# A layer norm, attention and GELU layer on one core: another order of the first stage's tasks, and head stacks in one tile

## Chip, core and metric

The kernel runs on one core of a Trainium2 chip, as one program. The metric is the device time of one execution in microseconds (us). The engines are named as in the profile: PE is TensorE's matmul, PEld its weight loads, DVE is VectorE, ACT ScalarE, POOL GpSimd; SP (SyncE) issues every DMA of this kernel, in program order, and its queue appears as SPq.

## What is computed

x has 2048 rows of 512 values, there are 32 heads of 16, and the feed-forward part has 1792 hidden units. One layer norm feeds both branches:

```python
xn = _layernorm(x)                                   # no weights
qkv = xn @ wqkv                                      # 512 -> 3 * 512, heads of 16
p = softmax(q @ k.T * 16 ** -0.5);  att = (p @ v) @ wo
h = gelu(xn @ w1 + b1);             mlp = h @ w2 + b2
return x + att + mlp
```

## The kernel before

Values are kept as pairs of f16 numbers (a high and a low part), so that a product of two of them is three matmuls (`PAIRS`). Q and K of a head are written to a DRAM tensor `qk_d` with three copies of parts per value, and read back as *stacks*: 48 rows (16 values by 3) for each of the four heads of a group, in the tiles `qst` and `kst`. Rows 62 and 63 of each half of a `qst` tile hold the negated row maxima of the scores, split in two, so that the second score product already has the maximum taken off. There are 8 groups of 4 heads (`g`), 4 query blocks of 512 (`qb`), and 16 units in each, so 512 units `u`; `t = 4 g + qb` counts the *turns* of 16 units.

A unit has two halves of the softmax. `s_half` makes scores with the queries in the partitions (`pS`) and DVE takes their maxima (line 330, four a unit). When a turn is through, `store` turns the maxima with PE, writes them to `m_d` in DRAM and reads them back into the stack's rows (lines 361 and 366). LEAD = 19 units later `e_half` makes the same scores with the keys in the partitions (`pT`), ACT takes the exponential (line 381, four a unit), and `v_half` sums with V (`pV`). Between these, a unit holds some products of a filler (`pD`): the rest of the V and QK projections, then the MLP, then the output projection, in this order, each as soon as its inputs are there. A filler group of 12 products in two halves takes three units at pace 4. At the change from the projections to the MLP, and again to the output projection, `flush` puts out all that is still queued for POOL and SP. From the MLP on, `more_stacks` issues one block's stack of the group after next in each unit, until its eight are out.

The first stage runs ahead of the units. It loads x and the weights, normalises (`normal`, line 896 and what follows), turns x with PE (line 928), projects the first Q and K (`project0`, line 958) and 11 of 16 V tiles (`v_tile`, line 1053), sends Q and K through DRAM into the stacks (line 990), and makes the scores of the first 19 units. Its tasks are put into an order by `Plan`: each task has an engine, a guessed duration, what it comes after and a `tail`, and `run` always takes, of the tasks that could begin first, the one with the longest tail. Every engine then keeps that order. Where the plan sees a gap on PE ahead of the first score, `fill` puts in matmuls that only keep PE busy (line 1122).

Lines that the change touches: `project0` (958 to 990), `v_tile` (1053), the turn of the first maxima (1081 to 1093), the stacks (480 and 990), `store` (361, 366), the load of `b1` (1127), and the generator `rest`, which lists the filler of the first blocks. After the stage, `prepare` begins on DVE with the maximum of `b1` (line 1165).

Of the kernel before, what the change touches and what calls it, by code (L numbers as in the profile page):

```python
# [18 lines left out]
P = 128  # L19
# [3 lines left out]
DH = 16  # L23
# [14 lines left out]
NV = 11  # L38
VT = 2600, 8000
FINE = "fine"  # L40
# [10 lines left out]
def layer_kernel(ctx: ExitStack, tc: tile.TileContext, x, wqkv, wo, w1, b1, w2, b2, out):  # L51
# [4 lines left out]
    def pool(stack, name, bufs=1, space=None, side=None):  # L56
# [22 lines left out]

    kst, qst = ([[[const.tile([P, QB], F16, name=f"{x}st{i}_{p}_{b}") for b in range(NQB)] for p in range(2)]  # L80
                 for i in range(2)] for x in "kq")

    def clear(i, blocks=range(NQB)):
        for b in blocks:
            for p in range(2):
                nc.gpsimd.memset(kst[i][p][b].bitcast(F32), MROWS)
                nc.gpsimd.memset(qst[i][p][b].bitcast(F32), 0.0)

# [117 lines left out]
    class Plan:  # L206
# [97 lines left out]
    def flush():  # L304

        settle()
        while steps or extras or any(q[2] for q in queue):
# [4 lines left out]
            slot[0] += 1  # L312

    def s_mm(u, n, s):
# [7 lines left out]
        tiled(None, s, qs[p][qb][r, qt * P:(qt + 1) * P], ks[p][kb][r, :], True, True)  # L322

# [15 lines left out]
    def s_end(u):  # L339
# [4 lines left out]
        g, qb = divmod(t, NQB)  # L344
        qs = qst[g % 2]
        mneg = mnegs[t % 2]
# [3 lines left out]
        def store():  # L350

            pt = banks("S")
            for a in range(2):
                nc.tensor.matmul(pt[32 * a:32 * a + 32, :64], mneg[64 * a:64 * a + 64, :],
                                 ident[64 * a:64 * a + 64, 64 * a:64 * a + 64], start=True, stop=True)
            mhl = work.tile([64, 2, 64], F16, name="mhl", bufs=2)
            nc.vector.tensor_scalar_mul(mhl[:, 0], pt[:64, :64], 1.0 / MROW)
            nc.vector.scalar_tensor_tensor(mhl[:, 1], pt[:64, :64], 1.0 / MROW, mhl[:, 0], op0=ALU.mult, op1=ALU.subtract)
            given("dve", 300)
            for a in range(2):  # L360
                nc.sync.dma_start(m_d[t, :, :, 64 * a:64 * a + 64], mhl[32 * a:32 * a + 16])
            for p in range(2):
                for a in range(2):
                    h = 2 * p + a
                    dst = qs[p][qb][64 * a + 62:64 * a + 64, :].rearrange("r (t q) -> r t q", q=P)
                    nc.sync.dma_start(dst, m_d[t, 4 * h:4 * h + 4].rearrange("t r q -> r t q"))

        stores[t] = store

    def e_half(u, n):  # L370
# [6 lines left out]
        k0 = (kt % 4) * P  # L377
        tiled(None, st, kst[g % 2][p][kt // 4][r, k0:k0 + P], qst[g % 2][p][qb][r, :], True, True)
        pe = work.tile([P, QB], F32, name="pe", bufs=12)
# [93 lines left out]
    NU = NG * NQB * 16  # L473

    def stacks(g, w, blocks):
        for b in blocks:
            for p in range(2):
                for a in range(2):
                    h = 4 * g + 2 * p + a
                    nc.sync.dma_start((qst, kst)[w][g % 2][p][b][64 * a:64 * a + 48, :],  # L480
                                      qk_d[w, h * DH:(h + 1) * DH, :, b * QB:(b + 1) * QB].rearrange("d j n -> (d j) n"))


# [68 lines left out]

    def project(m, w, sb, wh, bank, early=False):

# [5 lines left out]
        def finish(pj):  # L560
            def put():
                nc.sync.dma_start(dst[:, w:w + 2, :], stg)
                nc.sync.dma_start(dst[:, 2 - 2 * w, :], stg[:, 0])

            stg = ph.tile([P, 2, QB], F16, name="stg", bufs=3)
            given("act", 600)
            if early or (w == 1 and not m):
                nc.scalar.activation(stg[:, 0], pj, AF.Copy)
                nc.vector.tensor_tensor(stg[:, 1], pj, stg[:, 0], op=ALU.subtract)
            else:  # L570
                pf = ph.tile([P, QB], F32, name="pf", bufs=2)
                nc.scalar.activation(pf, pj, AF.Copy)
                if not m:
                    nc.scalar.activation(stg[:, 0], pj, AF.Copy)
                    nc.gpsimd.tensor_tensor(stg[:, 1], pf, stg[:, 0], op=ALU.subtract)
                else:
                    hi = lambda: nc.gpsimd.tensor_scalar(stg[:, 0], pf, 1.0, 0.0, op0=ALU.mult, op1=ALU.add)
                    lo = lambda: nc.gpsimd.tensor_tensor(stg[:, 1], pf, stg[:, 0], op=ALU.subtract)
                    later(1, lambda: pooled((620, hi), (1160, lo), (0, lambda: later(2, put, True))), True)
                    return  # L580

            put()

# [188 lines left out]
    with ExitStack() as st1:  # L772
# [48 lines left out]
        def tile_in(t):  # L821
            def fn():
                xs[t] = raw(("xs", t), "xs", [P, D], 8)
                nc.sync.dma_start(xs[t], x[t * P:(t + 1) * P, :])
# [11 lines left out]
        def piece_in(key, src, after=()):  # L836
# [3 lines left out]
            return add("SP", 420, fn, after, take=[key], size=700)  # L840

# [40 lines left out]
        wvv = wqkv[:, 2 * D:3 * D].rearrange("(c p) n -> p c n", p=P)  # L882
        v_in = [piece_in(("wch", "v", i), wvv[:, :, i * W:(i + 1) * W]) for i in range(2)]
        x_in += [tile_in(t) for t in range(4, NT)]
# [4 lines left out]
        def normal(sb):  # L889
# [18 lines left out]
            for i in range(4):  # L908
                v = 4 * sb + i
                if i >= DVE_X[sb]:  # L910
                    out.append(add("ACT", 620, lambda v=v, i=i: nc.scalar.activation(
                        xs[v], xs[v], AF.Identity, scale=sd[:, 2, i:i + 1], bias=sd[:, 4, i:i + 1]), [b]))
# [49 lines left out]
        def project0(w, sb):  # L962
# [23 lines left out]
            got = []  # L986
            for p_ in range(2):
                for a_ in range(2):
                    h_ = 2 * p_ + a_
                    got.append(add("SP", 420, lambda p_=p_, a_=a_, h_=h_: nc.sync.dma_start(  # L990
                        (qst, kst)[w][0][p_][sb][64 * a_:64 * a_ + 48, :],
                        qk_d[w, h_ * DH:(h_ + 1) * DH, :, sb * QB:(sb + 1) * QB].rearrange("d j n -> (d j) n")), [a, b], size=48))
            return got
# [46 lines left out]
        for i in range(2):  # L1040
            hi, lo = (wvh[j][:, :, i * W:(i + 1) * W] for j in range(2))
            key = ("wch", "v", i)
            h = add("ACT", 1040, lambda hi=hi, key=key: nc.scalar.activation(hi, tl[key], AF.Copy, scale=inv_v[:, 0:1]), [chain])
            wv_ready.append(add("DVE", 1200, lambda hi=hi, lo=lo, key=key: nc.vector.scalar_tensor_tensor(
                lo, tl[key], inv_v[:, 0:1], hi, op0=ALU.mult, op1=ALU.subtract), [h], free=[key]))

# [43 lines left out]
        for k in range(4):  # L1090
            def fn(k=k):
                dst = qst[0][k // 2][0][64 * (k % 2) + 62:64 * (k % 2) + 64, :].rearrange("r (t q) -> r t q", q=P)
                nc.sync.dma_start(dst, m_d[0, 4 * k:4 * k + 4].rearrange("t r q -> r t q"))
            add("SP", 270, fn, put, size=4)
# [38 lines left out]
        def rest():  # L1133
# [318 lines left out]
```

## Time and profile before

| | us |
|---|---|
| median of 3 runs (1506.58 to 1510.22) | 1507.2 |
| the profiled execution's own time | 1507.74 |
| its span | 1506.0 |
| PE busy | 1475.0 (98%) |
| DVE busy | 1376.2 (91%) |
| ACT busy | 1266.5 (84%) |
| POOL busy | 662.8 (44%) |

PE's busy time counts a matmul as busy also while it runs at half clock, and matmuls overlap, so the share alone does not tell where time is lost. The number of exponentials in a stretch does: four are a unit. The stage before the units ends with the first `pT` matmul at about 99.9 us.

### The profile page before, as it was taken

How to read it: one execution, taken by the hardware profiler on the slowest of the kernel's cores; microseconds unless marked ns; L12 is line 12 of the kernel's file. 1: busy time of each engine (PE TensorE's matmuls, PEld its weight loads, DVE VectorE, ACT ScalarE, POOL GpSimd, SP SyncE). 2: the span in 40 equal slices, each digit the busy share in tenths (PEclk: the TensorE clock that was granted, in tenths of full speed). 3: DMA queues.
4: the chain of work that ended last, by engine and by line, in shares of the span. 5: the costliest groups of instructions: out<-in, count | busy, mean ns of one | idle time of the engine just before them, and what ended most of it. 6: DMA issues, size and time to landing. Idle time of an engine off the chain costs nothing.

```text
span 1506.0 us, 87998 instructions
## 1 busy us (share of the span) xinstructions
PE 1475.0 (98%) x40055; PEld 814.7 (54%) x40055; DVE 1376.2 (91%) x2306; ACT 1266.5 (84%) x2367; POOL 662.8 (44%) x687
## 2 busy tenths in 40 slices
PE   8989999998999999999999999999999999999998
PEld 4435555554555555555555555555555555555554
DVE  7779989998999999999999999999999999999923
ACT  6748888887899888899988889998888999888884
POOL 3201979423677411278731137873105777211210
PEclk8999999999999999999999999999999999999999
DMA  6741677223222211131121111121112210111432
GB/s 214 226 150 41 208 223 232 85 85 100 83 86 76 80 50 30 41 83 36 51 57 49 44 50 37 46 79 57 30 36 56 65 43 21 48 53 39 131 99 93
DMA packets 114414, 124.82 MB, mean 83 GB/s; under 512 B 24700, under 2 KB 86012, under 8 KB 114040
## 3 DMA queue, kind: packets, MB, share of 16 engines
q1 hardware_dynamic: 114040, 119.19, 26.5%
q8 instruction: 313, 5.13, 1.4%
q14 instruction: 61, 0.50, 0.1%
HBM read 81.66 MB, written 37.34 MB: 79 GB/s over the span
## 4 chain that ended last, share of the span: by engine, by line
PE 86%; DVE 8%; DMA 3%; issue 1%; ACT 1%; SPq 1%; DVEq 0%; ACTq 0%
PE pV L167 25%; PE pD L167 22%; PE pS L167 18%; PE pT L167 18%; DVE mt L330 7%; PE pT L958 2%; DMA m_d<-mhl 1%; DMA xs<-in_A_x_dram 1%; PE pD L958 1%; DVE ac L1326 0%; PE pT L928 0%; DMA qst<-m_d 0%; DVE bs L896 0%; DVE mneg L347 0%; SPq L990 0%
## 5 line engine op out<-in xcount | busy, mean ns | idle before, releaser
L330 DVE TENSOR_REDUCE mt<-pS 128x1 f32<-128x512 f32 x2029 | 1297.3, 684 | 60.8 <-PE pS L167 36.4
L381 ACT ACTIVATE pe<-pT 128x512 f32<-128x512 f32 x2048 | 1111.8, 599 | 191.8 <-PE pT L167 86.2
L167 PE MATMUL pV<-pe,vv 64*32 64x512 f32 x8192 | 1073.4, 595 | 0.7 <-issue 0.6
L167 PE MATMUL pT<-qst,kst 64*32 64x512 f16 x8192 | 711.8, 379 | 6.6 <-DMA qst<-m_d 5.5
L167 PE MATMUL pS<-kst,qst 62*32 62x512 f16 x8116 | 617.8, 379 | 9.2 <-DVE mt L330 6.1
L167 PEld LDWEIGHTS <-qst 62*32 62x32 f16 x8192 | 277.9, 92 | 230.5 <-issue 58.9
L167 PEld LDWEIGHTS <-kst 64*32 64x32 f16 x8192 | 278.9, 91 | 180.2 <-issue 77.7
L167 PE MATMUL pD<-xb,wc 64*32 64x512 f16 x5376 | 361.6, 378 | 0.0
L167 PE MATMUL pD<-w_s,g 64*32 64x512 f16 x5376 | 359.1, 377 | 0.0
L167 PEld LDWEIGHTS pV<-pe,vv 64*32 64x32 f32 x8192 | 181.8, 105 | 87.7 <-PE pV L167 2.7
L167 PE MATMUL pD<-xt,wqk_h 64*32 64x512 f16 x2304 | 151.0, 378 | 0.3 <-issue 0.3
L167 PEld LDWEIGHTS <-wc 64*32 64x32 f16 x5376 | 117.1, 92 | 42.6 <-issue 0.3
L167 PEld LDWEIGHTS <-g 64*32 64x32 f16 x5376 | 113.1, 91 | 44.2
L1294 POOL TENSOR_TENSOR xa<-xa,yt 128x512 f32<-128x512 f32 x16 | 20.4, 1277 | 242.4 <-ACT yt L1292 242.4
L437 POOL TENSOR_TENSOR osb<-osb,rb 128x512 f32<-128x512 f32 x31 | 39.9, 1287 | 171.8 <-DMA rb<-den_d 116.5
L1249 POOL TENSOR_TENSOR t<-hh 128x512 f32<-128x512 f32 x56 | 58.2, 1040 | 76.9 <-ACT hh L1269 76.0
L1251 POOL TENSOR_TENSOR t<-t,hh 128x512 f32<-128x512 f32 x56 | 71.8, 1283 | 4.7
L1244 POOL TENSOR_TENSOR t<-t,hh 128x512 f32<-128x512 f32 x56 | 71.8, 1282 | 4.7
L1246 POOL TENSOR_TENSOR g<-t,g 128x512 f16<-128x512 f32 x56 | 65.2, 1164 | 4.7
L1243 POOL TENSOR_SCALAR t<-t,gs 128x512 f32<-128x512 f32 x56 | 38.7, 691 | 56.9 <-ACT t L1238 56.6
L167 PEld LDWEIGHTS <-wqk_h 64*32 64x32 f16 x2304 | 51.8, 92 | 20.4 <-issue 2.2
L167 PE MATMUL pD<-wo_s,oc 64*32 64x512 f16 x732 | 48.2, 378 | 0.0
(160 smaller groups left out, 891.7 us busy)
## 6 DMA issues: line engine op xcount, KB each, us to landing
wch<-in_B_w_dram SPq DMA_DIRECT2D x28, 512.0 KB
wc<-w_d SPq DMA_DIRECT2D x56, 256.0 KB
qk_d<-stg SPq DMA_DIRECT2D x32, 256.0 KB
rb<-den_d SPq DMA_DIRECT2D x124, 64.0 KB
w_d<-wsp SPq DMA_DIRECT2D x28, 256.0 KB
kst<-qk_d SPq DMA_DIRECT2D x128, 48.0 KB
qst<-qk_d SPq DMA_DIRECT2D x128, 48.0 KB
xs<-in_A_x_dram SPq DMA_DIRECT2D x16, 256.0 KB
```

Source lines behind the costliest of these rows:

```text
L167: p = nc.tensor.matmul(*args, **kw)
L330: nc.vector.reduce_max(mt_of[t][:, n, qt, kb:kb + 1], s, axis=AX.X)
L381: nc.scalar.activation(pe, st, AF.Exp, scale=scale_of[g // 2])
L437: pooled((1280, lambda: nc.gpsimd.tensor_tensor(osb, osb, rb, op=ALU.mult)), (620, lambda: nc.gpsimd.tensor_scalar(ot[:, 0], osb, 1.0, 0.0 ...
L958: nc.tensor.matmul(tl[key], lhs, rhs, start=c + n == 0, stop=(c, n) == (NC - 1, 2))
L1243: pooled((690, lambda: nc.gpsimd.tensor_scalar(t1, t1, 1.0, gs[:, 1:2], op0=ALU.add, op1=ALU.mult)), (1280, lambda: nc.gpsimd.tensor_tenso ...
L1244: (1280, lambda: nc.gpsimd.tensor_tensor(t1, t1, hh, op=ALU.mult)),
L1246: (1160, lambda: nc.gpsimd.tensor_tensor(g[:, 1, f, :], t1, g[:, 0, f, :], op=ALU.subtract)),
L1249: pooled((1040, lambda: nc.gpsimd.tensor_tensor(t1, hh, hh, op=ALU.mult)), (620, lambda: nc.gpsimd.tensor_scalar(t1, t1, 1.0, 1.0 / GELU_A ...
L1251: (1280, lambda: nc.gpsimd.tensor_tensor(t1, t1, hh, op=ALU.mult)),
L1294: add = lambda: nc.gpsimd.tensor_tensor(xa, xa, yt, op=ALU.add)
```

## The change

Four things are changed together.

1. **Stacks.** `kst` and `qst` get one tile for both head pairs, [128, 2, 512] instead of two of [128, 512]. A block's stack then comes in two transfers of 96 KB (one for each half of the partitions) where there were four of 48 KB. The clearing of the tiles is two memsets a block instead of four.
2. **The first stage's order.** The plan's delay for a transfer goes from 1800 to 3000 ns, its engines begin at given times rather than at 0, and several tasks get tails: the first x tiles, the QK and V weights, the low parts of the V weights, the rows of the first maxima; V tiles get a smaller one. `fill` puts its matmuls in smaller gaps and counts them otherwise.
3. **`b1`** is loaded in the first stage, after the ninth x tile, rather than at its end.
4. **One Q projection** (group 0 and 1, query block 3) is taken out of the first stage. It stands in the filler after the V tiles, and its stack is issued two slots after its result is written.

```diff
+LAG, E_TAIL = 3000, 8000
-VT = 2600, 8000
+VT = 2600, -2000
+WV_TAIL, WV_DVE = 50000, 2
...
-    kst, qst = ([[[const.tile([P, QB], F16, name=f"{x}st{i}_{p}_{b}") for b in range(NQB)] for p in range(2)]
-                 for i in range(2)] for x in "kq")
+    kst, qst = ([[const.tile([P, 2, QB], F16, name=f"{x}st{i}_{b}") for b in range(NQB)] for i in range(2)] for x in "kq")
...
-                    wire = 1800 + a["size"] * 3 if a["size"] else 0
+                    wire = LAG + a["size"] * 3 if a["size"] else 0
...
-            at = {e: 0.0 for e in ("PE", "ACT", "DVE", "POOL", "SP")}
+            at = {"PE": 1200.0, "ACT": 2020.0, "DVE": 1200.0, "POOL": 4000.0, "SP": 740.0}
...
+    def stack(g, w, b, a):
+        rows = qk_d[w, 4 * g * DH:(4 * g + 4) * DH, :, b * QB:(b + 1) * QB].rearrange("(p a d) j n -> a (d j) p n", p=2, a=2)
+        nc.sync.dma_start((qst, kst)[w][g % 2][b][64 * a:64 * a + 48], rows[a])
+
     def stacks(g, w, blocks):
         for b in blocks:
-            for p in range(2):
-                for a in range(2):
-                    h = 4 * g + 2 * p + a
-                    nc.sync.dma_start((qst, kst)[w][g % 2][p][b][64 * a:64 * a + 48, :],
-                                      qk_d[w, h * DH:(h + 1) * DH, :, b * QB:(b + 1) * QB].rearrange("d j n -> (d j) n"))
-
+            for a in range(2):
+                stack(g, w, b, a)
...
             def put():
                 nc.sync.dma_start(dst[:, w:w + 2, :], stg)
                 nc.sync.dma_start(dst[:, 2 - 2 * w, :], stg[:, 0])
+                if not m:
+                    later(2, lambda: stacks(0, w, [sb]), True)
...
-            return add("SP", 420, fn, take=[("xs", t)], size=256)
+            return add("SP", 450, fn, take=[("xs", t)], size=256, tail=(300000 if t < 4 else 270000 if t < 8 else 0))
...
-            return add("SP", 420, fn, take=[key], size=256)
+            return add("SP", 420, fn, take=[key], size=256, tail=0 if m else 290000)
...
-        q_ready[3] = project0(0, 3)
...
+        add("SP", 420, lambda: nc.sync.dma_start(b1_s, b1.rearrange("(f p) -> p f", p=P)), x_in[8:9], size=100)
...
         def fill(a, b):
-            if b - a > 700 and not s_of:
-                for _ in range(int((b - a - 250) / WARM)):
+            if b - a > 500 and not s_of:
+                for _ in range(int((min(b, 7000) - a) / 430) if a < 7000 else int((b - a - 200) / 215)):
                     nc.tensor.matmul(wp, wvh[0][:, 0, 0:P], wvh[0][:, 0, :], start=True, stop=True)
...
-        nc.sync.dma_start(b1_s, b1.rearrange("(f p) -> p f", p=P))
...
             for t in range(NV, NT):
                 yield v_group(t, wvh, dbank)
+            yield project(0, 0, NQB - 1, wqh, dbank)
```

What the plan makes of it is seen in the order of the engines' instructions. Line numbers are those of each kernel's own file: 990 and 480 before are 479 after, 1053 is 1048, 381 is 383.

First, SP from the fifth load of x to the first stacks, before. `stg` is a projection's result on its way to `qk_d`; the numbers in a stack's name are the head pair, the block and a counter.

```order
L824 DMA xs<-in_A_x_dram 128x512 x4
L833 DMA wq<-in_A_wqkv_dram 128x4x128 x2
L985 DMA qk_d<-stg 128x512 x2
L984 DMA qk_d<-stg 128x2x512 x2
L824 DMA xs<-in_A_x_dram 128x512 x4
L990 DMA kst_0_0_79<-qk_d 48x512 x2
L990 DMA kst_1_0_83<-qk_d 48x512 x2
L990 DMA qst_0_0_95<-qk_d 48x512 x2
L990 DMA qst_1_0_99<-qk_d 48x512 x2
```

The same stretch of SP after, where a stack's name has only the block and a counter.

```order
L817 DMA xs<-in_A_x_dram 128x512 x8
L826 DMA wq<-in_A_wqkv_dram 128x4x128 x2
L1099 DMA b_s<-in_B_b_dram 128x14x1
L978 DMA qk_d<-stg 128x512 x2
L977 DMA qk_d<-stg 128x2x512 x2
L479 DMA kst_0_79<-qk_d 48x2x512 x2
L479 DMA qst_0_87<-qk_d 48x2x512 x2
L817 DMA xs<-in_A_x_dram 128x512 x4
```

The load of `b1` (`b_s`) now stands ahead of the first results, and the last four x tiles have moved behind the first stacks.

Second, ACT at the end of the first stage, up to the first exponentials (`pe`), before: `vv` is the copy of a finished V tile, `wch,amx` the sum over a piece of a weight, `stg` and `pf` the two copies of a Q projection.

```order
L847 ACTIVATE wch,amx<-wch 128x1024 x2
L1053 ACTIVATE vv<-pT 128x32x16
L847 ACTIVATE wch,amx<-wch 128x1024
L970 ACTIVATE stg<-pT 128x512
L980 ACTIVATE pf<-pT 128x512
L970 ACTIVATE stg<-pT 128x512
L980 ACTIVATE pf<-pT 128x512
L381 ACTIVATE pe<-pT 128x512 x14
```

The same stretch after.

```order
L1048 ACTIVATE vv<-pT 128x32x16
L840 ACTIVATE wch,amx<-wch 128x1024 x4
L963 ACTIVATE stg<-pT 128x512
L973 ACTIVATE pf<-pT 128x512
L1048 ACTIVATE vv<-pD 128x32x16
L840 ACTIVATE wch,amx<-wch 128x1024
L1048 ACTIVATE vv<-pT 128x32x16 x2
L383 ACTIVATE pe<-pT 128x512 x14
```

Two Q projections stood last before; now one does, and three V tiles come behind it.

Third, SP where the filler goes from the projections to the MLP, in the turn before group 2 begins, before. `wc` is a piece of w1; `m_d` is the store of the maxima of turn 6. Four stack issues for `kst_0_0` and `kst_1_0` stand just ahead.

```order
L480 DMA kst_0_1_80<-qk_d 48x512 x2
L480 DMA kst_1_1_84<-qk_d 48x512 x2
L621 DMA wc<-w_d 128x1024
L480 DMA kst_0_2_81<-qk_d 48x512 x2
L480 DMA kst_1_2_85<-qk_d 48x512 x2
L480 DMA kst_0_3_82<-qk_d 48x512 x2
L480 DMA kst_1_3_86<-qk_d 48x512 x2
L480 DMA qst_0_0_95<-qk_d 48x512 x2
L480 DMA qst_1_0_99<-qk_d 48x512 x2
L480 DMA qst_0_1_96<-qk_d 48x512 x2
L480 DMA qst_1_1_100<-qk_d 48x512 x2
L361 DMA m_d<-mhl 32x1x64 x2
```

The same place after, from the last part of the filler's projections.

```order
L435 DMA rb<-den_d 32x512 x4
L564 DMA qk_d<-stg 128x2x512
L565 DMA qk_d<-stg 128x512
L564 DMA qk_d<-stg 128x2x512
L565 DMA qk_d<-stg 128x512
L479 DMA kst_0_79<-qk_d 48x2x512 x2
L479 DMA kst_1_80<-qk_d 48x2x512 x2
L614 DMA wc<-w_d 128x1024
L479 DMA kst_2_81<-qk_d 48x2x512 x2
L366 DMA m_d<-mhl 32x1x64 x2
L318 DMA qst_2_93<-m_d 2x4x128 x4
L479 DMA kst_3_82<-qk_d 48x2x512 x2
```

The store of turn 6's maxima has 6 stack issues behind the filler's last results where it had 24. The other blocks' stacks come behind it.

More of the change, by code (lines that the diff above doesn't have):

```diff
@@ L312, in flush, with m_rows @@
             slot[0] += 1
+    def m_rows(t, h):
+        g, qb = divmod(t, NQB)
+        p, a = divmod(h, 2)
+        dst = qst[g % 2][qb][64 * a + 62:64 * a + 64, p].rearrange("r (t q) -> r t q", q=P)
+        nc.sync.dma_start(dst, m_d[t, 4 * h:4 * h + 4].rearrange("t r q -> r t q"))
     def s_mm(u, n, s):
@@ L344, in s_end @@
         g, qb = divmod(t, NQB)
-        qs = qst[g % 2]
         mneg = mnegs[t % 2]
@@ L563, in put @@
                 nc.sync.dma_start(dst[:, 2 - 2 * w, :], stg[:, 0])
+                if not m:
+                    later(2, lambda: stacks(0, w, [sb]), True)
             stg = ph.tile([P, 2, QB], F16, name="stg", bufs=3)
             given("act", 600)
[L567 to L582, printed above, removed]
+            pf = ph.tile([P, QB], F32, name="pf", bufs=2)
+            nc.scalar.activation(pf, pj, AF.Copy)
+            hi = lambda: nc.gpsimd.tensor_scalar(stg[:, 0], pf, 1.0, 0.0, op0=ALU.mult, op1=ALU.add)
+            lo = lambda: nc.gpsimd.tensor_tensor(stg[:, 1], pf, stg[:, 0], op=ALU.subtract)
+            later(1, lambda: pooled((620, hi), (1160, lo), (0, lambda: later(2, put, True))), True)
         return Group(prods, bank, finish)
@@ L839, in fn @@
                 nc.sync.dma_start(tl[key], src)
-            return add("SP", 420, fn, after, take=[key], size=700)
+            return add("SP", 420, fn, after, take=[key], size=700, tail=tail)
         def total(ns, key, dst, after, done=()):
@@ L910, in normal @@
                 if i >= DVE_X[sb]:
-                    out.append(add("ACT", 620, lambda v=v, i=i: nc.scalar.activation(
+                    out.append(add("ACT", 710, lambda v=v, i=i: nc.scalar.activation(
                         xs[v], xs[v], AF.Identity, scale=sd[:, 2, i:i + 1], bias=sd[:, 4, i:i + 1]), [b]))
@@ L986, in project0 @@
             got = []
[L987 to L992, printed above, removed]
+            for a_ in range(2):
+                got.append(add("SP", 420, lambda a_=a_: stack(0, w, sb, a_), [a, b], size=96))
             return got
@@ L1091, in fn @@
             def fn(k=k):
-                dst = qst[0][k // 2][0][64 * (k % 2) + 62:64 * (k % 2) + 64, :].rearrange("r (t q) -> r t q", q=P)
-                nc.sync.dma_start(dst, m_d[0, 4 * k:4 * k + 4].rearrange("t r q -> r t q"))
-            add("SP", 270, fn, put, size=4)
+                m_rows(0, k)
+            add("SP", 270, fn, put, size=4, tail=E_TAIL)
         for t in range(NV):
```

32 lines of the change are left out of this document (17 added, 15 removed).

## Prediction

> **What bounds the kernel now.** I read the page first, then the busy time of stretches around the end of the first stage and around a dip of PE at 370 us, then the count of exponentials in the same stretches (four are a unit), and last the chain of waits and the timeline at the places that stood out. The page's first two lines:
>
> ```profile
> span 1506.0 us, 87998 instructions
> PE 1475.0 (98%) x40055; PEld 814.7 (54%) x40055; DVE 1376.2 (91%) x2306; ACT 1266.5 (84%) x2367; POOL 662.8 (44%) x687
> ```
>
> PE and DVE share the bound, so a gain has to come from stretches in which both stand. Busy time by stretch (start and end, length, busy of each engine, granted clock, DMA share, GB/s):
>
> ```profile
> 0.00:33.90 33.90, 27.16 (x125) 13.92 (x126) 25.91 (x76) 23.02 (x41) 12.26 (x44) 0.90 0.72 227
> 33.90:93.50 59.60, 58.87 (x480) 23.14 (x483) 46.06 (x87) 40.30 (x76) 10.34 (x9) 0.97 0.63 196
> 93.50:99.90 6.40, 2.88 (x41) 0.76 (x40) 5.26 (x11) 1.47 (x4) 2.27 (x2) 0.91 0.37 128
> 99.90:105.50 5.60, 5.59 (x92) 2.77 (x97) 2.63 (x4) 2.97 (x6) 0.00 (x0) 0.50 0.48 82
> 105.50:110.00 4.50, 3.47 (x87) 1.47 (x84) 3.79 (x10) 2.37 (x5) 0.00 (x0) 1.00 0.47 117
> ```
>
> From 33.9 to 93.5 PE has no gap. From 93.5 to 99.9 it works 2.88 of 6.40 us, and right after it the units begin at half clock. Exponentials (ACT busy and count, clock, DMA) show what that and the dip cost:
>
> ```profile
> 100.50:126.20 25.70, 17.50 (x33) 0.90 0.33 85
> 126.20:147.90 21.70, 17.39 (x32) 1.00 0.16 46
> 354.00:368.00 14.00, 11.11 (x22) 1.00 0.44 121
> 368.00:382.00 14.00, 5.65 (x11) 0.88 0.31 88
> ```
>
> The first eight units take 25.7 us, the next eight 21.7. At 368 a stretch of 14 us yields half its units: 7 us are lost there. SP's queue tells why:
>
> ```profile
> 353.46 0.38 SPq L562 DMA_DIRECT2D qk_d<-stg  x1
> 353.89 1.75 SPq L563 DMA_DIRECT2D qk_d<-stg  x1
> 355.74 4.53 SPq L480 DMA_DIRECT2D kst<-qk_d  x8
> 360.32 0.42 SPq L621 DMA_DIRECT2D wc<-w_d  x1
> 360.84 4.95 SPq L480 DMA_DIRECT2D kst<-qk_d  x8
> 365.84 5.08 SPq L480 DMA_DIRECT2D qst<-qk_d  x8
> 371.02 1.23 SPq L361 DMA_DIRECT2D m_d<-mhl  x2
> 373.48 1.15 SPq L366 DMA_DIRECT2D qst<-m_d  x4
> ```
>
> ```profile
> 363.87 0.22 DVE L358 SCALAR_TENSOR_TENSOR mhl<-pS,mhl 64x64 f16<-64x64 f32 x1
> ...
> 375.06 0.63 PE L167 MATMUL pT<-qst,kst 64*32 64x512 f16 x8 [4.47 <-DMA qst<-m_d]
> ```
>
> The maxima are ready at 364.1 and stored from 371.0, because 24 stack issues at 0.6 us stand ahead; PE waits 4.47 us for the rows.
>
> **The change, part by part.**
>
> *Stacks (D).* From the filler's change on, one block's stack is issued a unit: four issues of 0.6 before, two after. SP comes late to the first of them, because the filler's last results stand ahead and wait for POOL, and before, a block's 2.4 us of issues in a unit of 2.7 us (21.7 / 8) let it catch up hardly at all: six units' stacks and a `wc` are the 15.3 us from 355.74 to 371.02, six units 16.2 us, so SP was 6.9 + 0.9 = 7.8 us late at the first stack and 6.9 at the store. PE waited 4.5 of these 6.9, so a store that is 2.4 us late costs nothing. After, the filler ends three units later, and three units' stacks and a `wc` stand ahead of the store, 7 x 0.6 = 4.2 us against 8.1 us of units. SP is then 7.8 + 4.2 - 8.1 = 3.9 us late and PE waits 1.5: D = -(7.0 - 1.5) = -5.5. An issue of 96 rows is not in the trace. Its bounds are one of 48 rows (0.6) and two of them (1.2, by which SP is 7.5 us late and D is 0); I take 0.6, as the 128 rows of `qk_d<-stg` took 0.38. D lies between -7 and 0. In all other units no PE wait stands behind the stacks, and I cost them at nothing there: they are due many units ahead.
>
> *End of the first stage (A).* Counted in the order, PE has the same work between the first score and the first exponential before and after: 308 score matmuls, 180 projection matmuls, 32 turns. (One Q projection goes out, but another moves from ahead of the first score to behind it.) Only its place changes: three V tiles (36 matmuls) now end behind the last Q projection, between the last scores, where before PE had scores alone and waited for DVE's maxima. Before, the work took 99.9 - 33.9 = 66.0 us, in which PE was busy 58.87 + 2.88 = 61.75. Clock 0.97 over 59.6 us is 3.6 us at half clock, 1.8 us lost, which dense work ahead would save: 60.0. DVE's 46.06 + 5.26 = 51.3 us stay below. So A is -6.0 if PE never waits and 0 if DVE's maxima come late again; I allow 1 us of waits and take -5.
>
> *The first score (B).*
>
> ```profile
> 24.86 0.46 SPq L824
> ...
> 26.41 5.57 DMA xs<-in_A_x_dram
> 32.00 1.85 DMA qst<-qk_d
> 33.89 0.62 PE pV L167 x3
> ```
>
> The chain to the first scores goes through the last four x tiles, 1 MB that SP issues from 24.86 ahead of the stacks. After, the stacks stand ahead of them. Without them the result's write and the stack are two steps like the 1.85, and the last stack stands three issues of 0.46 behind: 24.9 + 2 x 1.85 + 1.4 = 30.0, at most 3.9 us sooner. Against it speaks the start:
>
> ```profile
> 3.95 0.63 ACT L847 ACTIVATE wqk_h<-wq 128x512 f32<-128x512 f32 x1 [1.94 <-DMA wq<-in_A_wqkv_dram]
> ...
> 5.60 1.28 ACT L900 ACT_TABLE_LOAD   x1
> ...
> 6.46 0.70 DVE L896 BATCH_NORM_STATS2 bs<-xs 128x6 f32<-128x512 f32 x1 [5.33 <-DMA xs<-in_A_x_dram]
> ...
> 10.36 0.21 ACT L900 ACTIVATE sd<-sd 128x4 f32<-128x4 f32 x1 [3.47 <-DVE sd L898]
> ```
>
> x comes first now, some 2.5 us sooner (6.46 less 3.95), but ACT's order puts the sum over the first QK weight, which lands fifth, and the table load of 1.28 ahead of the square root, so that this stays near 10. PE's order has 8 filling matmuls between the turns of x and the first projection, and 17 more behind it; at the full-clock rate of the next fence (0.65 for 3) these are 1.7 and 3.7 us, at half clock the 8 are 3.4. `b1`, which now stands ahead of the first results in SP's queue, is 3.10 us of transfer there at worst. Loss up to 4 us. I take B = 0, between -3.9 and +4.
>
> *The units' start (C).* Half clock for the 5.6 us from 99.9 costs 2.8. DVE waits for `b1`:
>
> ```profile
> DVE am_all L1165 <- DMA b_s<-in_B_b_dram: 2.2, 1, 2.2
> ```
>
> Both together are the 25.7 against 21.7 x 33 / 32 = 22.4: 3.3 us. With V tiles between the last scores PE stays busy and the clock stays; `b1` is there long before. C = -3.3, at least -0.5 from `b1` alone. A rule to weigh: the Trainium skill (TensorE: Matmul & The Clock Gate, Part 1: The HAM clock gate) says that one busy window of about 3.4 us releases the clock. By it half clock would have cost 1.7 instead of 2.8 and the sum would be 1.1 us smaller; the row shows 0.50 for 5.6 us of nearly full PE work and decides.
>
> *The Q projection in the blocks (E).* It is 12 products:
>
> ```profile
> 64.37 0.65 PE pT L958 x3
> ...
> 1494.51 1.91 PE L167 MATMUL pS<-wo_s,oc 64*32 64x512 f16 x60
> ...
> 1498.61 2.75 PE L512 MATMUL pD<-wo_l,ot 64*128 64x512 f16 x12
> ```
>
> The number of filler products in a unit is fixed, so everything behind shifts three units, and the last three units' worth ends up behind the last unit, where PE still works filler off (the x60 row) and nothing hides it: 12 x 0.65 / 3 = +2.6 us. Nothing would be hidden at best (0, if it fell into the DVE steps there), and three whole units (8.1) at worst; the work's own length is nearest. Its POOL copies and its transfers join queues that have a group like it every three units. Its stack has a due time:
>
> ```profile
> 167.61 0.45 SPq L562 DMA_DIRECT2D qk_d<-stg  x1
> ...
> 186.78 1.25 SPq L361 DMA_DIRECT2D m_d<-mhl  x2
> 191.73 1.16 SPq L366 DMA_DIRECT2D qst<-m_d  x4
> ```
>
> The first filler projection's result is written at 167.6. The moved one takes that place; two units later (173) its stack comes up in SP's queue, and a landing took up to 191.73 - 186.78 = 5 us in this stretch, so it is there by 178 to 183, one landing for the write or none, and one for the stack. The block's first score stands in the unit of the store at 186.8: 4 us or more are left.
>
> Memsets (half as many, the same bytes, on POOL, ahead of everything) go at nothing.
>
> Sum: -5.5 - 5 + 0 - 3.3 + 2.6 = -11.2 us against the profiled execution's 1507.7, 1496.5. The median, 1507.2, is 0.5 below that execution: 1496.0.
>
> **Rivals.** (1) The late store stays or moves. For it: SP must still get through what the filler's end puts out at once, and with issues of 1.2 us nothing is gained. Against: 18 issues fewer. With D = 0, 1501.5. (2) The first stage keeps its loose end. For it: scores of the last key block wait for a projection, a write and a stack, and 18 V matmuls in a row stand ahead of these scores, while DVE runs out; the work behind is then bound by 28 maxima. PE still idles and the clock drops. A = 0, C = -1: 1496.0 + 5 + 2.3 = 1503.3. (3) Slower: one tile for both pairs makes the first exponential score of a turn wait for all four rows of maxima rather than for its own pair's. That is in 31 turns; at 1 us each it is +31, 1527, and it makes the kernel slower by more than 0.3% from (11.2 + 4.5) / 31 = 0.51 us a turn. Against it: the four issues are 1.15 us together, half of that is what a turn would add, and 2.4 us of slack stand before it. (4) The stage begins later: B = +4 alone gives 1500.0, inside the range.
>
> **How the numbers follow.** 0.3% of 1507.2 is 4.5 us, about what a measurement can tell from no change. Forecast 0.58 (1496.0; with terms off by a few us, 1490 to 1501), rival 1 0.17, rival 2 0.13, both at once 0.05 (1508.8), rival 3 0.07. Faster, below 1502.7: nearly all of the forecast (0.56), three quarters of rival 1 (0.13) and half of rival 2 (0.07, its terms being no firmer than the others), 0.76. Slower, above 1511.7: rival 3 and 0.04 of mishaps over several terms, 0.11. The rest, 0.13, is within. The low end has B, A and D at their best: 1496.0 - 3.9 - 1 - 1.5 = 1489.6. The high end takes in rivals 1 and 2 and stops short of both together, 1507.
>
> **What would show it.** D: no idle of PE on `qst<-m_d` above 1 us near 365, and full counts of exponentials there. A and C: first `pT` at 93 to 96, clock 1.00 in the 6 us behind it, no DVE wait on `b_s`. B: first scores at 30 to 38. E: some 2.6 us more between the last unit and the end. I am wrong if the first `pT` still comes at 99 behind an idle PE, if a wait for maxima appears in another turn, or if units of every turn's start grow.

## The result, and the profile after

The changed kernel takes 1497.05 us (median of 4 runs, 1494.62 to 1498.02), the kernel before in the same set of runs 1508.71 (1506.58 to 1511.35): a ratio of 0.9919, 95% interval 0.9897 to 0.9942. Measured once more in another set it was 1494.67 us, ratio 0.9916 (0.9895 to 0.9937). The forecast was 1496.0 with a range of 1489.6 to 1507.0. The profiled execution took 1498.02 us with a span of 1496.2; all terms below are taken from this profile and the one before.

The page's row for the matmuls that need a turn's maxima, after and then before (busy time and mean ns; idle time ahead of them and what ended most of it):

```profile
L167 PE MATMUL pT<-qst,kst 64*32 64x512 f16 x8192 | 713.2, 377 | 2.9 <-DMA qst<-m_d 2.9
...
L167 PE MATMUL pT<-qst,kst 64*32 64x512 f16 x8192 | 711.8, 379 | 6.6 <-DMA qst<-m_d 5.5
```

PE waits 2.9 us for maxima in the whole span, where it waited 5.5. Rival 3 needed 0.51 us in each of 31 turns, 15.8 us; it did not happen.

Busy time around the end of the first stage, after (stretch and length, busy of PE, PEld, DVE, ACT and POOL with counts, granted clock, DMA share, GB/s):

```profile
32.80:93.50 60.70, 59.94 (x521) 23.46 (x521) 53.27 (x103) 44.11 (x82) 11.37 (x10) 1.00 0.69 217
93.50:95.70 2.20, 0.82 (x29) 0.34 (x32) 1.35 (x4) 0.60 (x1) 0.00 (x0) 1.00 0.58 180
95.70:101.30 5.60, 5.60 (x153) 2.94 (x149) 5.59 (x13) 4.54 (x9) 0.00 (x0) 1.00 0.90 273
```

First scores stand at 32.8 us in both profiles. The first exponential moved from 100.6 to 95.7 us, and the 5.6 us behind it have a clock of 1.00. Before, the 5.6 us from the first `pT` had 0.50, and those from the first exponential 0.55. The loose end is not quite gone: PE still works only 0.82 of the last 2.20 us.

The exponentials divide the rest. The stretches below begin and end with the same exponential in both kernels (length; ACT busy and count; clock; DMA share; GB/s). Before:

```profile
100.50:126.10 25.60, 17.49 (x32) 0.90 0.33 85
126.10:147.90 21.80, 17.40 (x32) 1.00 0.16 46
147.90:194.10 46.20, 34.97 (x64) 1.00 0.63 195
194.10:284.60 90.50, 69.55 (x128) 1.00 0.64 201
284.60:375.70 91.10, 69.46 (x128) 1.00 0.30 90
375.70:463.20 87.50, 69.21 (x128) 0.98 0.27 79
463.20:1314.10 850.90, 694.59 (x1280) 1.00 0.18 51
1314.10:1486.80 172.70, 138.50 (x255) 1.00 0.25 73
```

After:

```profile
95.70:118.10 22.40, 17.35 (x32) 1.00 0.24 71
118.10:140.10 22.00, 17.40 (x32) 1.00 0.13 35
140.10:189.00 48.90, 34.82 (x64) 1.00 0.62 191
189.00:279.90 90.90, 69.74 (x128) 1.00 0.65 201
279.90:366.10 86.20, 69.61 (x128) 1.00 0.32 97
366.10:451.60 85.50, 69.34 (x128) 1.00 0.28 79
451.60:1302.10 850.50, 694.44 (x1280) 1.00 0.18 51
1302.10:1472.60 170.50, 138.18 (x255) 1.00 0.26 77
```

Line by line the difference is -3.2, +0.2, +2.7, +0.4, -4.9, -2.0, -0.4 and -2.2; ahead of them are the -4.8 of the earlier first exponential, and behind them +4.4, since 23.6 us are left after the last stretch instead of 19.2. That adds up to -9.8, the difference of the two spans.

The fifth line is the store of the maxima. SP's queue and VectorE at that place, after:

```profile
354.84 1.83 SPq L479 DMA_DIRECT2D kst<-qk_d  x4
356.72 0.43 SPq L614 DMA_DIRECT2D wc<-w_d  x1
357.25 2.26 SPq L479 DMA_DIRECT2D kst<-qk_d  x2
359.61 1.23 SPq L366 DMA_DIRECT2D m_d<-mhl  x2
362.24 1.14 SPq L318 DMA_DIRECT2D qst<-m_d  x4
...
359.20 0.22 DVE L363 SCALAR_TENSOR_TENSOR mhl<-pS,mhl 64x64 f16<-64x64 f32 x1
```

The maxima are ready at 359.4 and their store is issued at 359.6. From the first stack (354.84) to the store are 4.77 us, with six stack issues and a `wc`; one issue alone took 1.84 of the 2.26 us in the third row. Over the whole profile the middle issue of 96 rows takes 0.43 us, and the middle one of 48 rows in the profile before 0.42, with single ones of up to 2.0 and 1.9: of these two sizes, SP pays for the issue and not for the bytes.

The end is the line that grew. All of it behind the last exponential, before and after, and PE's last rows after:

```profile
1486.80:1506.00 19.20, 12.38 (x218) 4.98 (x202) 9.99 (x16) 1.85 (x4) 0.00 (x0) 0.97 0.44 166
```

```profile
1472.60:1496.20 23.60, 17.68 (x296) 7.49 (x280) 10.83 (x17) 1.89 (x4) 0.00 (x0) 0.96 0.36 135
...
1480.80 1.91 PE L167 MATMUL pS<-wo_s,oc 64*32 64x512 f16 x60
1482.83 3.90 PE L167 MATMUL pD<-wo_s,oc 64*32 64x512 f16 x64
```

PE has 5.3 us more to do there. The moved projection's twelve products are eight pieces each, and the 64 pieces of the second row are eight products' worth: 0.49 us a product. The row above it does 60 pieces in 1.91, half of that a product: it takes the two row halves in turn, while the second row does all pieces of one half and then all of the other (lines 701 to 710 of the changed kernel).

### The profile page after: what moved, and what is told of

It is laid out like the page before. It is cut to its first block, busy times and chain, and to the rows that moved or that the text cites. A ratio compares the mean times of both kernels' runs of the same rounds, so it can differ in the third digit from the quotient of the medians.

```text
span 1496.2 us, 88010 instructions
## 1 busy us (share of the span) xinstructions
PE 1473.7 (98%) x40140; PEld 819.1 (55%) x40140; DVE 1377.0 (92%) x2307; ACT 1265.1 (85%) x2365; POOL 661.0 (44%) x671
## 4 chain that ended last, share of the span: by engine, by line
PE 85%; DVE 10%; DMA 2%; ACT 1%; issue 1%; SPq 1%; POOL 0%; DVEq 0%; POOLq 0%; ACTq 0%
PE pV L167 25%; PE pD L167 23%; PE pS L167 18%; PE pT L167 17%; DVE mt L336 8%; PE pT L951 2%; DMA m_d<-mhl 1%; DMA wq<-in_A_wqkv_dram 1%; PE pD L951 1%; DVE ac L1321 0%; ACT xs L904 0%; DMA den_d<-dn 0%; SPq L1312 0%; DVE xt L934 0%; DMA rb<-den_d 0%
## 5 line engine op out<-in xcount | busy, mean ns | idle before, releaser
L167 PE MATMUL pD<-xt,wqk_h 64*32 64x512 f16 x2400 | 158.8, 378 | 1.1 <-issue 1.1
L167 PEld LDWEIGHTS <-g 64*32 64x32 f16 x5376 | 113.5, 91 | 43.9
L167 PEld LDWEIGHTS <-wqk_h 64*32 64x32 f16 x2400 | 55.1, 92 | 21.4 <-issue 3.4
```

The lines of the kernel that those rows point to most:

```text
L167: p = nc.tensor.matmul(*args, **kw)
```

## The experiments

Each set of runs has its own runs of the kernel before, so ratios are compared, not medians: 0.3% is 4.5 us, and the intervals are some 0.002 to each side. Where an effect has its own place in the trace, the profile tells more than the ratio.

**Stacks alone, and their absence.** The first takes the kernel before and changes only the tile and the transfers:

```diff
-            for p in range(2):
-                for a in range(2):
...
-                    nc.sync.dma_start((qst, kst)[w][g % 2][p][b][64 * a:64 * a + 48, :],
+            for a in range(2):
+                stack(g, w, b, a)
```

> The kernel before, with the shared tile and two transfers per stack as the only edit (in the first stage too, where the plan sees them). Theory (D is from the issues alone): the PE wait of 4.5 us near 370 us is gone, SP catches up over six units' stacks, 12 issues of 0.46; time 5 to 7 us below the kernel before, from the first exponential to the end; the first stage, whose plan may shift, stays within 2 us of 100.6. Rival: the wait stays, because POOL and the filler's results hold SP, not the stacks; the time of the kernel before within 1 us.

Measured: 1500.2 us, ratio 0.9942 (0.9926 to 0.9957). SP's queue at the store, and VectorE's last step ahead of it:

```profile
358.63 2.72 SPq L475 DMA_DIRECT2D kst<-qk_d  x4
361.39 1.86 SPq L475 DMA_DIRECT2D qst<-qk_d  x4
365.05 1.23 SPq L359 DMA_DIRECT2D m_d<-mhl  x2
...
364.80 0.22 DVE L356 SCALAR_TENSOR_TENSOR mhl<-pS,mhl 64x64 f16<-64x64 f32 x1
```

SP now idles from 363.3 until the maxima are there, and PE's wait of 4.5 us is gone: the turn with the dip takes 4.5 us less. The time fell by 9 us, more than forecast. In the profile the rest is 1.8 us in the first eight units (the first stage is planned anew, as the plan sees fewer transfers), 1.3 in the turn behind the dip and 2.4 in the last two turns (which vary, as shown further down), against 0.8 lost ahead of the first exponential and 1.4 in the second turn.

The second takes the changed kernel and splits the transfers again, in the blocks alone:

```diff
-            for a in range(2):
-                stack(g, w, b, a)
+            for p in range(2):
+                for a in range(2):
...
+                    nc.sync.dma_start((qst, kst)[w][g % 2][b][64 * a:64 * a + 48, p],
```

> The changed kernel, but each stack that is loaded inside the blocks goes as four transfers of 48 rows again (into the same shared tile); the first stage is untouched. Theory (the number of issues makes the store of the maxima late): three blocks' stacks stand ahead of the store near 360 us; 12 issues of 0.6 instead of 6 of 0.46 put it 4.4 us later, slack takes up to 2.4, so PE waits 2 to 4.5 us for the rows of maxima there and the time is 2 to 4.5 us above the changed kernel's 1497. Rival (it is the place of the filler's end, three units later, that removed the wait): no PE wait near 365 us above 1 us, and the changed kernel's time within 1 us.

Measured: 1504.03 us, ratio 0.9955 (0.9939 to 0.9971). The rows at the store, the time at which the maxima were ready, and PE's waits from 355 to 380 us (total, times, longest):

```profile
357.44 4.81 SPq L486 DMA_DIRECT2D kst<-qk_d  x8
362.81 1.77 SPq L486 DMA_DIRECT2D kst<-qk_d  x4
364.68 2.04 SPq L366 DMA_DIRECT2D m_d<-mhl  x2
...
361.81 0.22 DVE L363 SCALAR_TENSOR_TENSOR mhl<-pS,mhl 64x64 f16<-64x64 f32 x1
...
PE pT L167 <- DMA qst<-m_d: 1.2, 1, 1.2
```

The store is 2.7 us late and PE waits 1.2; the turn takes 88.1 - 86.2 = 1.9 us more for its pair. So issues make the store late, as the theory has it, but the later end of the filler would by itself have taken most of the 4.5 us away: the first of these stacks is issued 4.6 us before the maxima are ready, as in the changed kernel. Either half of the change nearly suffices, and they don't add up. The time, however, rose by 0.0036, some 5.5 us, more than the theory's place explains. Much of the rest stands at another store, that of the third turn's maxima. They are ready at 177.55 us and stored at 182.31, PE waits 5.4 us for them, and behind that wait the clock is 0.50 from 188.55 to 195.38. The changed kernel is late at that store too, by 2.2 us (see the transfers from 140 to 280 us). Its two stack issues ahead of it took 2.52 us and the four here 2.05, so their number does not explain the difference, and that part is not settled.

**The Q projection.** It goes back into the first stage:

```diff
         q_ready[2] = project0(0, 2)
+        q_ready[3] = project0(0, 3)
...
-            yield project(0, 0, NQB - 1, wqh, dbank)
```

> The changed kernel, but the fourth Q projection of the first heads is made in the first stage again and not in the blocks. Theory (its twelve products cost their length wherever PE is full; the order, not the shorter work, closed the gap at the first stage's end): the first exponential comes 2 to 3 us later than the changed kernel's 95.7, clock 1.00 after it, the part behind the last exponential is 4.4 us shorter (19.1), and there is no wait for maxima near 365 us; time 1 to 3 us below the changed kernel's 1497. Rival (the gap closed because this projection went out): the first exponential is back at 99 to 101 with a clock of 0.5 behind it, and the time is 1 to 4 us above the changed kernel's.

Measured: 1493.7 us, ratio 0.9891 (0.9875 to 0.9907). The first exponential comes at 98.6 (2.9 us later). The stretch around it, and the one behind the last exponential:

```profile
98.50:104.10 5.60, 5.60 (x153) 2.96 (x149) 5.56 (x13) 4.48 (x9) 0.00 (x0) 1.00 0.90 270
...
1476.60:1495.70 19.10, 12.31 (x218) 4.92 (x198) 9.93 (x16) 1.78 (x4) 0.00 (x0) 0.97 0.44 167
```

The clock stays at 1.00 with the projection in its old place, so the order, not the shorter first stage, closed the gap. The second row is the 19.2 us and the 218 matmuls of before. So the projection costs 2.9 us in the first stage and 4.4 at the end: by these two places, moving it was a loss of 1.5 us. The ratios do not settle it, as their intervals overlap, and in this profile, the slowest of five executions, turns 7 and 9 take 3.4 us more than in the changed kernel (43.9 and 44.9 against 42.7 and 42.7), for a reason that was not found.

**The V tiles.** One number of the plan, the urgency of the V tiles, goes back:

```diff
-VT = 2600, -2000
+VT = 2600, 8000
```

> The changed kernel with one number of the plan put back, the urgency of the V tiles in the first stage: the V matmuls move ahead of the last Q projection, and 44 score matmuls in a row stand at the end, where the changed kernel has V matmuls between the last scores (30 V and 44 score matmuls). Theory (A and C are these V matmuls: they keep PE busy while VectorE takes the maxima, and with it the clock): first exponential at 99 to 101 instead of 95.7, PE idle 2 to 4 us ahead of it, granted clock 0.5 to 0.7 in the 6 us behind it, and the time 4 to 8 us above the changed kernel's 1497. Rival (A comes from the other numbers of the plan): first exponential within 1.5 us of 95.7 and the time within 1.5 us.

Measured: 1502.17 us, ratio 0.994 (0.9919 to 0.9962). The stretch behind the first exponential, which now comes at 99.5 us:

```profile
99.50:105.10 5.60, 5.60 (x128) 2.94 (x116) 4.33 (x10) 3.89 (x8) 0.00 (x0) 0.74 0.91 278
```

The first exponential is 3.8 us later and the first eight units take 23.7 instead of 22.4 us, with the clock at 0.74. That is 5.1 of the 8.0 us which A and C gained together: the V matmuls between the last scores are the mechanism of most of both. The intervals of the two ratios overlap, so it is the trace that shows this.

The 0.74 is a cut out of a longer spell at half clock, from 95.58 to 102.41 us. In the profile before, the spell is 98.68 to 105.51 us, 6.83 us long as well. Its two halves, before and then here:

```profile
98.68:102.09 3.41, 2.79 (x44) 1.06 (x48) 1.85 (x3) 1.09 (x2) 0.00 (x0) 0.50 0.24 67
102.10:105.51 3.41, 3.41 (x60) 1.80 (x56) 1.29 (x2) 1.90 (x4) 0.00 (x0) 0.50 0.58 83
...
95.58:98.99 3.41, 1.44 (x20) 0.36 (x23) 3.17 (x6) 0.00 (x0) 0.00 (x0) 0.50 0.42 130
99.00:102.41 3.41, 3.41 (x60) 1.65 (x48) 1.67 (x3) 1.41 (x3) 0.00 (x0) 0.50 0.77 216
```

In both, PE idles in a part of the first half and has no gap in the second.

**The load of b1.** It goes back behind the first stage:

```diff
-        add("SP", 420, lambda: nc.sync.dma_start(b1_s, b1.rearrange("(f p) -> p f", p=P)), x_in[8:9], size=100)
...
         wfs[1] = [tl["wq", 1, w] for w in range(2)]
+        nc.sync.dma_start(b1_s, b1.rearrange("(f p) -> p f", p=P))
```

> The changed kernel, but the load of b1 stands behind the whole first stage in SP's queue, as before. Theory: VectorE waits about 2.2 us for it again among the first units, which PE and VectorE cannot make up; 1 to 2.5 us above the changed kernel's 1497. Rival: the first units have room for it, since PE is no longer at half clock there; within 0.5 us of the changed kernel.

Measured: 1496.4 us, ratio 0.9916 (0.9894 to 0.9938): no difference. VectorE does not wait for it at all in this profile, and the first eight units take 22.8 us against 22.4. So the late load costs nothing in the changed kernel; whether its 2.2 us were a cost in the kernel before was not run.

**The filler's pace at the end.** Three groups of the last block's hidden products go faster:

```diff
-                             for c in range(NC) for i, j in PAIRS], dbank, hidden, pace=FAST if f % 2 else SLOW)
+                             for c in range(NC) for i, j in PAIRS], dbank, hidden, pace=FAST if f % 2 or (b == NQB - 1 and f < 6) else SLOW)
```

> The changed kernel, but three groups of the last block's hidden products go at the faster pace of eight half products a unit instead of six, so that all filler behind them comes three units sooner. Theory (E: the moved projection's twelve products lie bare behind the last unit, while a unit with more filler costs 0.1 to 0.2 us): the part behind the last exponential falls from 23.5 to 19 to 20 us, the turns with the faster groups grow by 0.5 to 1 us, and the time is 2 to 4 us below the changed kernel's 1497. Rival (a unit is bound by PE there, so that filler costs its length at either place): the end is shorter and the turns longer by the same; the time within 1 us.

Measured: 1494.55 us, ratio 0.9891 (0.987 to 0.9912). The last 256 exponentials, behind which 19.3 us are left:

```profile
1300.70:1474.40 173.70, 138.39 (x256) 1.00 0.25 73
```

The end is 4.3 us shorter, but these exponentials take 173.7 us where the changed kernel took 170.5, and the turn with the faster groups 0.9 more: 4.1 us given back. From the 257th exponential to the end both profiles have 1216.3 us. The ratio alone would have called it a gain; the run below with the same pace did not confirm that. This speaks for the rival without proving it: 3.0 of the 4.1 us stand in the last two turns, which vary (86.4 and 84.8 us in two profiles of the changed kernel; 89.4 here and 89.1 in the run below).

**The transfers from 140 to 280 us.** The third stretch grew by 2.7 us, which no term had. At its place stands the store of the third turn's maxima. VectorE's last step ahead of it, the store, its rows, and PE's waits from 140 to 285 us:

```profile
178.49 0.22 DVE L363 SCALAR_TENSOR_TENSOR mhl<-pS,mhl 64x64 f16<-64x64 f32 x1
180.87 1.24 SPq L366 DMA_DIRECT2D m_d<-mhl  x2
186.86 1.15 SPq L318 DMA_DIRECT2D qst<-m_d  x4
...
PE pT L167 <- DMA qst<-m_d: 1.6, 1, 1.6
PE pS L167 <- issue: 1.3, 1, 1.3
PE pD L167 <- issue: 1.1, 2, 0.8
PE pV L167 <- issue: 1.1, 2, 0.6
```

The maxima are ready at 178.7, so SP is 2.2 us late here, as it was 6.9 us late at 371 us in the kernel before: its queue has no free moment ahead of this store, and the prediction put the stacks there at nothing. Then the rows follow the store only after 6.0 us. Three of the four wait lines name no releaser. First the weights' copying was spread out:

```diff
                 while not ended[0] or len(v_done) < NT:
                     yield
+                yield
                 ended[0] = False
```

> The changed kernel, but the copying of the MLP's weights (load, split on POOL, write back) pauses one more unit after each of its 16 pieces; the same pieces, spread over some 43 us more. Theory (the unforeseen loss between 140 and 280 us is transfers of this copying, behind which the maxima's store lands 5 us late, 1.6 us of PE wait at 187 us, and PE's pauses without a named releaser): the second to fourth turn take 44 to 46 us each instead of 48.9, 46.1 and 44.8, and the time is 2 to 5 us below the changed kernel's 1497. Rival (these pauses have nothing to do with the transfers): the same turns within 1 us, the time within 1 us.

Measured: 1495.13 us, ratio 0.9897 (0.9873 to 0.9921). The second to fourth turn take 44.7, 43.5 and 48.7 us: the loss went from the second turn to the fourth, and the three together take 136.9.

> Both edits together: the fourth Q projection in the first stage again, and the copying of the weights with a pause after each piece. Theory: what was measured with the projection in the first stage (1493.7, and 4.4 us less behind the last exponential) and 2 to 5 us less in the second to fourth turn add up, 1489 to 1492. Rival: the two overlap, since that kernel's profile had no wait for maxima at 187 us; 1493 to 1495.

Measured: 1495.17 us, ratio 0.9893 (0.9872 to 0.9914): the gains do not add up.

Then writes were withheld from the two units ahead of a store:

```diff
+    def calm(n, fn):
+        def step():
+            if pos[0] % 16 in (14, 15, 0):
+                later(1, step, True)
+            else:
+                fn()
+        later(n, step, True)
...
-                later(10 + 3 * k, lambda c=c, cols=cols: nc.sync.dma_start(xn_d[:, :, c, cols], xt[:, :, c, cols]), True)
+                calm(10 + 3 * k, lambda c=c, cols=cols: nc.sync.dma_start(xn_d[:, :, c, cols], xt[:, :, c, cols]))
...
-                            later(a, lambda a=a: nc.sync.dma_start(w1_d[n, :, a], wh[:, a]), True)
+                            calm(a, lambda a=a: nc.sync.dma_start(w1_d[n, :, a], wh[:, a]))
```

> The changed kernel, but no write of the copied weights and of the normalized input (128 to 256 KB each) is issued in the two units ahead of a turn's store of the maxima; they come after it. Theory (the store near 181 us stands behind some 1.5 MB issued in the 5 us ahead of it, and at some 300 GB/s that is its 5 us): the rows of maxima follow their store within 3 us, no PE wait for them above 0.5 us in the second to fourth turn, these three turns together 135 to 137 us, against 139.8 in the changed kernel's first profile. Rival (the 512 KB loads, which stay, hold the store, or the wait is not the queue's): the store still lands 4 us or more late, the three turns within 138 to 141 us.

Measured: 1496.92 us, ratio 0.9927 (0.9908 to 0.9946). The store and its rows:

```profile
177.84 1.36 SPq L376 DMA_DIRECT2D m_d<-mhl  x2
181.96 1.14 SPq L328 DMA_DIRECT2D qst<-m_d  x4
```

The maxima are ready at 177.8, so the store is not late, the rows follow in 4.1 us instead of 6.0, and PE waits for maxima no more. In the second profile of the changed kernel (the last run of this section), with nothing withheld, the store is 1.0 us late, the rows follow in 4.8, and PE waits 0.7 in all. One profile each can thus only suggest that the queue's content is a part of that delay. And PE now pauses 4.7 us without a releaser, and the three turns take 138.7 us: nothing is gained.

> The same withholding of writes, with the fourth Q projection in the first stage. Theory: 1 to 3 us below the same kernel without it (1493.7 there), that is a ratio of 0.987 to 0.9885 to the kernel before. Rival: that kernel had no wait for maxima, so nothing changes, 0.989.

Measured: 1493.48 us, ratio 0.9909 (0.9889 to 0.9929), not below the same kernel without the withholding (0.9891).

> The same withholding of writes, with the three faster filler groups of the last block. If the faster filler is worth nothing, as the sum of the turns in its profile says (the end 4.2 us shorter, the turns with it 4 us longer), its time is that of the withholding alone; if its measured ratio of 0.9891 was the truth, 2 to 4 us below it.

Measured: 1496.2 us, ratio 0.9929 (0.9908 to 0.9949), the time of the withholding alone (0.9927): no gain of the faster filler is seen.

> The changed kernel itself on the same chip, to compare the others with, and to see which pauses between 140 and 280 us repeat. Theory (they depend on when transfers land): the second to fourth turn differ by 1 us or more from the 48.9, 46.1 and 44.8 of its first profile, while the turns from the tenth on agree within 0.2 us.

Measured: 1494.67 us, ratio 0.9916 (0.9895 to 0.9937). The second turn, and the third and fourth, in this profile of the same program:

```profile
140.20:185.40 45.20, 34.83 (x64) 1.00 0.66 209
185.40:276.20 90.80, 69.68 (x128) 1.00 0.63 201
```

45.2 us, where the first profile had 48.9. The 2.7 us were one draw of a stretch that varies from execution to execution, while of the 28 turns behind it 25 agree within 0.1 us.

No version beats the changed kernel for certain. With the Q projection in the first stage the ratio was lower in each of three pairs (0.9891 against 0.9919 and 0.9916; 0.9893 against 0.9897; 0.9909 against 0.9927), by 0.6 to 4 us, with intervals that overlap.

## Why the prediction was right, by its terms

The time is 1 us from the forecast, but not every term is, and that it is so near is partly luck: 1.8 us of E and 3.1 in the second to fourth turn are set off by 1.4 more from D and 2.2 in the last turns.

- **A**, -5 forecast, -4.8 found. V tiles between the last scores did most of it: putting back their urgency alone brought 3.8 of it back. The allowance of 1 us for waits was 1.4 (PE idle 93.9 to 95.2).
- **B**, 0 forecast, 0 found: 32.8 us in both. (The 33.9 from which the prediction counts is the second group of scores.)
- **C**, -3.3 forecast, -3.2 found. The clock is most of its cause: 0.55, 0.74 and 1.00 in the 5.6 us from the first exponential go with 25.6, 23.7 and 22.4 us for the first eight units. From the first exponential on, half clock lasts 4.9 us before and 2.9 with the early V tiles, which costs 2.5 and 1.4 of the 3.2 and 1.3 us. Its lower bound, 0.5 from `b1` alone, found no support: with `b1` late nothing was lost in the changed kernel. There is also the rule weighed there (the Trainium skill, TensorE: Matmul & The Clock Gate, Part 1: one busy window of about 3.4 us releases the clock). The traces agree with it: the clock came back after 3.41 us in which PE had no gap, both before and with the early V tiles. The prediction read its row as speaking against the rule, but a stretch in which PE still idled (2.79 and 1.44 of 3.41 us busy) stood ahead of that one, which makes the spell 6.83 us; where PE was busy for 3.35 of 3.41 us at once (33.83 to 37.24, before), the spell was 3.41.
- **D**, -5.5 forecast, -4.9 found in its turn and -2.0 in the two turns behind. The mechanism was right and one size was off: how late SP is at the first stack. The prediction carried over the 7.8 us of before. Measured, the first stack is issued 4.6 us before the maxima are ready, so SP is 8.1 - 4.6 = 3.5 us late there. The 4.8 us from there to the store are near the 4.2 forecast, and so SP is 0.2 us late at the store instead of 3.9. Why it is less late where the filler now ends is not shown. By the prediction's sum four issues at the new place would have gained nothing (7.8 + 13 x 0.6 - 8.1 = 7.5 us late); measured they are 2.7 late. The runs show that two transfers at the old place remove the whole wait and four at the new one most of it.
- **E**, +2.6 forecast, +4.4 found. This is the term that was mis-sized. It was priced by a row of full 128-row products (0.22 us each), but the filler's last products run in pieces of 64 rows, one row half after the other, at 0.49 us each by the x64 row. The prediction's own fence had a row for that: 12 pieces of 64 rows in 2.75 us, 0.23 each, so 0.46 for the two halves of a product.
- **Not foreseen**: +3.1 in the second to fourth turn and -2.2 in the last four. The same program showed 139.8 and 136.0 us for those three turns, so one profile cannot price them. In the first profile, 1.6 us are the wait at the third turn's store, in units where D's working put the stacks at nothing.

Rivals 1 and 2, the store and the loose end that stay, did not come true; rival 3 is refuted by 2.9 us of waits in all; of rival 4 nothing was seen. The working treated the change as three gains, one term of nothing and one cost, and the runs bear that out: by places, the order gave 8.0 us (A and C), the store 6.9 (D), and the moved projection took 4.4 back. By ratios the two transfers alone give 0.0058 and the rest without them in the blocks 0.0045, together more than the whole (0.0081), since at the store either would nearly do.

## What to carry to other kernels

Follow a late wait back through the issuing queue and ask what stands ahead of the late transfer; halving the number of issues removed the whole 4.5 us wait here, where moving the work left 1.2. Price moved work by the form in which it runs at its new place, not by the form that it leaves. Before an unexpected stretch of a few microseconds is explained, profile the same program twice: if it moves, one profile cannot put it down to the edit.

## What was not expected of the hardware

- SP takes as long to issue a stack transfer of 96 rows in two segments as one of 48 rows: 0.43 us for the middle one of 128 after, 0.42 for the middle one of 256 before. Single issues of either kind take up to 2.0 and 1.9 us.
- In the first 200 us of all 14 profiles every spell at half clock lasts 3.41 or 6.83 us.
- From 140 to 280 us, with DMA at some 200 GB/s, PE pauses 0.3 to 1.7 us at a time with no releaser in the trace, 0.9 us in all before, 3.5 in the first profile after and 4.7 with the writes withheld, each time at other places. Spreading the transfers only moved the pauses. No run isolates their cause, but the DMA records point to one. The 14 profiles have 58 such pauses of over 0.3 us behind the first 130 us, and all of them end 1.2 to 1.6 us after the end of a transfer of the instruction queue (q8 on the page), of which there is one every 4.4 us (the middle of all distances). So PE probably waits for its own instructions there.
- The maxima's store, two transfers of 4 KB, holds up its reader for 4.1 us from its issue in that stretch with the writes withheld (177.84 to 181.96) and 6.0 in the changed kernel (180.87 to 186.86), and for 2.6 at 360 us (359.61 to 362.24).
